# K, V and wo loads issued from GpSimd instead of SyncE in a decode attention kernel

## The chip, the cores and the metric

The kernel runs on one core of a Trainium2 chip. The metric is the device time of one execution in microseconds, as the median of several runs. The profile is one more execution, recorded by the hardware profiler.

## What is computed

Two independent blocks, A and B, of the same shape: one new token for each of two sequences attends over a cache of 8192 keys in 32 heads of width 192. The two results are laid side by side.

```python
B, Sq, D = 2, 1, 640;  H, Sk, Dh = 32, 8192, 192          # all bf16
q = (x @ wq).reshape(B, Sq, H, Dh).transpose(0, 2, 1, 3)
scores = einsum("bhqd,bhkd->bhqk", q, k_cache) * Dh ** -0.5
p = softmax(scores, axis=-1)
o = einsum("bhqk,bhkd->bhqd", p, v_cache)
block = o.transpose(0, 2, 1, 3).reshape(B, Sq, H * Dh) @ wo
out = concatenate([block_A, block_B], axis=-1)
```

Each K and V element is read once, and the two caches of the two blocks are 805 MB of the 837 MB that are read.

## The kernel before

The work is cut into 64 units (`NU`). A unit is one pair of heads of one sequence: head one of the pair lies on partitions 0 to 63, head two on 64 to 127, and each partition holds 128 keys. Its K, and likewise its V, is one transfer of 128 rows of 48 KB, 6144 KB in all.

The transfers go into three buffers (`kv`, buffers 0 to 2 inside the tile `big`), taken in turn in the order of the list `loads`: K0, K1, V0, K2, V1, K3, V2 and so on, and V63 at the end. A load may begin when the load three places before it in the list has been used up (`done(i - NBUF)`): a K is used up when the last of its four multiplies has ended, a V when its PV matmuls have ended. So K(u+2) waits for PV of unit u-1, V(u+1) waits for the last multiply of K(u+1), and K2 waits for the last multiply of K0. K1 and V0 instead wait for the q matmuls of the first and the second block (`("pq", PPB * i - 1)`), because wq of both blocks lies where buffers 1 and 2 will be.

All loads are issued by SyncE in one order: wq of A, x of A and B, wq of B, K0, then the rest of `loads`, then wo in six pieces that go into the same buffers as these come free, then the two outputs.

What the engines do for unit u:

- VectorE multiplies K by q, which is spread over the partitions, in four chunks of 32 keys (`dve_mul`, L285). It reduces what TensorE has summed (`dve_red`, L289), takes the maximum of the scores in each partition (`dve_max`, L295), and finishes the sums of unit u-2 (L300 to L306).
- TensorE sums 192 products to 16 by twelve matmuls with the identity for each chunk (`pe_sum`, L362), then does the 64 PV matmuls of unit u-1 (`pe_pv`, L376).
- GpSimd takes the maximum over the partitions (`pool_ar`, L266, the all-reduce), once for each unit. Before the loops it fills constants.
- ScalarE makes the bias, the exponentials and the scaled outputs (L315, L324, L309).

The order of each engine's instructions comes from the tables `tabs`: `put(engine, slot, order, function, waits, signal)` enters an instruction, and at the end each engine's entries are sorted by slot, then by order. The slot is mostly the unit. SyncE has no table; its instructions run in the order in which they were added to `S_sp`. GpSimd's all-reduce of unit u has slot u and order 0. An engine runs its instructions strictly in order; a wait holds all that follow it.

A transfer adds 16 to a semaphore when it has landed. Before, each of the three buffers has one semaphore (`bsem`), and each load of it waits for the next multiple of 16.

At the start, q of all heads is made by TensorE from x and wq (`pe_q`, L354) and spread by VectorE and ScalarE (L275, L280); at the end wo is applied (`pe_out`, L404).

Of the kernel before, what the change touches and what calls it, by code (L numbers as in the profile page):

```python
# [117 lines left out]
def build_kernel(nc, blocks, out):  # L118
# [15 lines left out]
    NU = NP * B  # L134
    LASTU = NU - 1
    scale = float(Dh) ** -0.5
    NBUF = 3
# [9 lines left out]
    with ExitStack() as es:  # L147
        sb = lambda name, shape, dt: es.enter_context(nc.sbuf_tensor(name, shape, dt))
        ps = lambda name, shape, dt: es.enter_context(nc.psum_tensor(name, shape, dt))
        sem = lambda name: es.enter_context(nc.semaphore(name))  # L150
# [42 lines left out]
        reg = {}  # L193
        S_sp = _Stream("sp", sem("s_sp"), reg)
# [1 line left out]
        S_act = _Stream("act", sem("s_act"), reg)  # L196
        S_dve = _Stream("dve", sem("s_dve"), reg)
        S_pool = _Stream("pool", sem("s_pool"), reg)
        bsem = [sem(f"bsem{i}") for i in range(NBUF)]

        def dsem(k, n=1):
            reg[k] = (sem("d_" + "_".join(str(i) for i in k)), 16 * n)
# [6 lines left out]
        loads = [("k", 0)]  # L209
# [1 line left out]
            loads += [("k", u), ("v", u - 1)]  # L211
        loads += [("v", LASTU)]
        buf = {}
        bcount = [0] * NBUF
        for i, (kind, u) in enumerate(loads):
            buf[kind, u] = i % NBUF
            bcount[i % NBUF] += 1
            reg[(kind, u)] = (bsem[i % NBUF], 16 * bcount[i % NBUF])

        bk, b62, b63 = buf["k", LASTU], buf["v", LASTU - 1], buf["v", LASTU]  # L220
        assert (bk, b62, b63) == (2, 0, 1)
# [1 line left out]
        pieces = []  # L223
        for blk, rows, off, w in ((0, (WR,), woA, [("s", LASTU, NCH - 1)]), (1, (29,), wo0, [("pv", LASTU - 1)]),
                                  (1, (11, 5, 2, 1), wo1, [("pv", LASTU)])):
            r = 29 if off == wo1 else 0
            for n in rows:
                pieces.append((blk, r, r + n, off, w))
                off, r, w = off + n * D, r + n, []
# [9 lines left out]
        def back(name, u, c, n):  # L239
            i = u * NCH + c - n  # L240
            return (name, i // NCH, i % NCH) if i >= 0 else None

        def dma(out_ap, in_ap, k):
            s = reg[k][0]
            return lambda eng: eng.dma_start(out_ap, in_ap).then_inc(s, 16)
# [8 lines left out]
        def ld_wo(n):  # L254
            blk, r0, r1, off, _ = pieces[n]
            src = blocks[blk]["wo"].rearrange("(p i) n -> p (i n)", i=WR)
            return dma(big[:, off:off + (r1 - r0) * D], src[:, r0 * D:r1 * D], ("wo", n))

        def ld_kv(kind, u):
            hp, b = u // B, u % B  # L260
            blk, h = hp // PPB, 2 * (hp % PPB)
            src = blocks[blk][kind][b, h:h + 2].rearrange("s (p t) d -> (s p) t d", p=64)
            return dma(kv[buf[kind, u]], src, (kind, u))
# [154 lines left out]
        def put(eng, slot, order, fn, waits, sig, tag=None):  # L418
            t = tabs[eng].setdefault(slot, [])
            t.append((order, len(t), fn, waits, sig, tag))  # L420
# [14 lines left out]
        for u in range(NU):  # L435
            for c in range(NCH):
                w = [("k", u), ("pq", NP - 1), ("qa", NP - 1), ("qx", NP - 1), back("s", u, c, 2)]
# [32 lines left out]
        for n, p in enumerate(pieces):  # L470
            w = [("wo", n), ("ot", p[0])]
# [8 lines left out]
        def done(i):  # L480
            if i < 0:
                return None
            kind, u = loads[i]
            return ("m", u, NCH - 1) if kind == "k" else ("pv", u)
# [5 lines left out]
        for i, (kind, u) in enumerate(loads):  # L490
            w = [done(i - NBUF)]
            if i in (1, 2):
                w = [("pq", PPB * i - 1)]
            S_sp.add(ld_kv(kind, u), waits=w)
        for n in range(len(pieces)):
            S_sp.add(ld_wo(n), waits=pieces[n][4])
        for blk in range(NBLK):
            S_sp.add(out_dma(blk), waits=[("oev", blk, 1), ("oev", blk, 0)])

# [2 lines left out]
        for n in range(1, HP + 1):  # L502
            S_pool.add((lambda n: (lambda eng: eng.memset(tri[0:n, n:n + 1], 1.0)))(n),
                       waits=[("tri0",)] if n == 1 else [], sig=("tri",) if n == HP else None)
# [5 lines left out]
        for n in range(128 // HP):  # L510
# [3 lines left out]
                  waits=[("id1",), ("place0",)], sig=("place",))  # L514
# [50 lines left out]
def bass_concat_heads__gqa_block_cached__mha_block_cached__decode_kernel(  # L565
    nc: bass.Bass,
    A_x: bass.AP,
    A_k_cache: bass.AP,
    A_v_cache: bass.AP,
    A_wq: bass.AP,  # L570
    A_wo: bass.AP,
    B_x: bass.AP,
    B_k_cache: bass.AP,
    B_v_cache: bass.AP,
    B_wq: bass.AP,
    B_wo: bass.AP,
    out: bass.AP,
):
    blocks = [
        dict(x=A_x, k=A_k_cache, v=A_v_cache, wq=A_wq, wo=A_wo),  # L580
        dict(x=B_x, k=B_k_cache, v=B_v_cache, wq=B_wq, wo=B_wo),
    ]
    build_kernel(nc, blocks, out)
# [28 lines left out]
```

## Time and profile before

| | |
|---|---|
| time before, median of 3 runs | 1937.1 us (1936.89 to 1937.25) |
| the profiled execution, span | 1936.0 us |
| bytes read from HBM | 836.77 MB, 432 GB/s over the span |
| DMA queue of SyncE (q1) | 99.9% of 16 engines' span |
| DMA issues by GpSimd | none |
| TensorE matmul busy | 1545.0 us (80%) |
| VectorE busy | 1124.0 us (58%) |
| GpSimd busy | 28.4 us (1%) |

The page gives the span of the profiled execution; what lies around it is the 1.1 us between the span and the median of the runs. Times in the rows are microseconds from the start of the span. In rows of the timeline the first two numbers are start and duration, the last bracket is how long the engine had been idle and what released it. SPq is SyncE's queue, which issues transfers; such a row lasts as long as the issuing, not the transfer. A row that groups several issues ("x2") reaches from the first to the end of the last. The last number of a row of the list of DMA issues is the median time from issue to landing.

### The profile page before, as it was taken

What the parts mean: (1) busy time and instruction counts of PE and PEld (TensorE: products, weight loads), DVE (VectorE), ACT (ScalarE), POOL (GpSimd) and SP (SyncE); (2) the same over time, 40 slices, a digit from 0 to 9 for tenths busy, and PEclk for the clock granted to TensorE, in tenths of its full rate; (3) what the DMA queues carried; (4) which work ended last, traced back from release to release, by engine and by line L of the source; (5) the groups of instructions that cost most, each with busy time, mean ns of one, the idle gap of its engine ahead of it and who ended that gap; (6) DMA issues with size and microseconds to landing.
All of it is one profiled execution on the core that took longest, in us unless ns stands there. A gap on an engine that the chain in (4) does not pass through costs nothing.

```text
span 1936.0 us, 19059 instructions
## 1 busy us (share of the span) xinstructions
PE 1545.0 (80%) x7728; PEld 743.0 (38%) x7729; DVE 1124.0 (58%) x907; ACT 142.3 (7%) x519; POOL 28.4 (1%) x113
## 2 busy tenths in 40 slices
PE   5777878878878878878878878878878878878878
PEld 2333434434434434434434434433433433433434
DVE  4765565565565565565565565565565565565560
ACT  3100000000000000000000000000000000000000
POOL 0000000000000000000000000000000000000000
PEclk9899989988989988989988999999999999999999
DMA  9999999999999999999999999999999999999999
GB/s 419 427 435 436 432 434 438 430 434 437 434 433 434 437 431 435 437 432 433 436 436 431 434 438 429 436 437 432 434 435 436 430 436 438 428 436 437 433 433 391
DMA packets 19610, 836.91 MB, mean 432 GB/s; under 512 B 2184, under 2 KB 2320, under 8 KB 2576
## 3 DMA queue, kind: packets, MB, share of 16 engines
q1 hardware_dynamic: 19600, 836.78, 99.9%
q8 instruction: 6, 0.10, 0.0%
q14 instruction: 4, 0.03, 0.0%
HBM read 836.77 MB, written 0.01 MB: 432 GB/s over the span
## 4 chain that ended last, share of the span: by engine, by line
DMA 49%; PE 31%; DVE 17%; issue 3%; DVEq 0%; SPq 0%; ACT 0%; ACTq 0%
DMA big<-in_B_k_cache_dram 24%; DMA big<-in_A_k_cache_dram 22%; PE ops L376 18%; DVE big L285 15%; PE scps L362 12%; DMA big<-in_B_wq_dram 2%; DVE sc L289 1%; DMA big<-in_B_wo_dram 1%; PE scps L354 0%; PE ops L368 0%; PE outps L354 0%; DVEq L285 0%; DVE qall L275 0%; PE scps L404 0%; PE oTps L390 0%
## 5 line engine op out<-in xcount | busy, mean ns | idle before, releaser
L285 DVE TENSOR_TENSOR big<-big,qall 128x6144 bf16<-128x6144 bf16 x256 | 852.7, 3351 | 490.7 <-DMA big<-in_B_k_cache_dram 260.6
L362 PE MATMUL scps<-big,ident 128*128 128x512 bf16 x3072 | 815.6, 426 | 358.2 <-DVE big L285 355.7
L376 PE MATMUL ops<-big,pb 128*34 128x384 bf16 x4096 | 676.8, 326 | 0.0
L362 PEld LDWEIGHTS scps<-big,ident 128*128 128x128 bf16 x3072 | 314.3, 107 | 852.7 <-DVE big L285 439.2
L376 PEld LDWEIGHTS ops<-big,pb 128*34 128x34 bf16 x4096 | 395.5, 98 | 258.7
L289 DVE TENSOR_REDUCE sc<-scps 128x32 f32<-128x512 f32 x256 | 175.9, 687 | 227.7 <-PE scps L362 227.7
L315 ACT ACTIVATE nb<-mg 64x1 f32<-64x1 f32 x128 | 25.8, 201 | 1707.7 <-POOL mg L266 1706.9
L324 ACT ACTIVATE pb<-sc,nb 64x128 bf16<-64x128 f32 x128 | 55.8, 436 | 7.8
L266 POOL PARTITION_ALL_REDUCE mg<-mp x64 | 25.7, 402 | 1859.1 <-DVE mp L295 1859.1
L295 DVE TENSOR_REDUCE mp<-sc 64x1 f32<-64x128 f32 x128 | 35.9, 280 | 8.3
L309 ACT ACTIVATE qall<-o_sum,rc 2x192 f32 (+1 forms) x64 | 29.0, 453 | 20.7 <-DVE o_sum L306 19.1
L306 DVE TENSOR_TENSOR o_sum<-ops,o_hi 2x192 f32<-2x192 f32 x64 | 22.1, 346 | 7.7
L354 PE MATMUL scps<-big,xw 128*128 x120 | 23.2, 351 | 2.6 <-DVE xw L271 2.2
L324 ACT ACTIVATION_READ_ACCUMULATOR pb<-sc,nb 64x1 f32 x128 | 23.7, 185 | 0.0
L303 DVE COPY o_hi<-ops 2x192 f32<-2x192 f32 x64 | 22.3, 349 | 2.0
L300 DVE RECIPROCAL rc<-ops 2x1 f32<-2x1 f32 x64 | 10.0, 156 | 21.3 <-PE ops L376 19.3
L275 DVE CAST qall<-scps 64x192 f32 x48 | 17.0, 355 | 7.2 <-PE scps L354 5.4
L280 ACT ACTIVATE qall<-scps 64x192 f32 x48 | 15.6, 324 | 30.5 <-DVE qall L275 28.2
L345 PE MATMUL oTps<-ident,xw 4*128 4x4 bf16 x5 | 0.4, 178 | 21.5 <-DMA xw<-in_B_x_dram 21.5
L354 PEld LDWEIGHTS scps<-big,xw 128*128 128x128 bf16 x120 | 12.4, 103 | 12.1 <-issue 5.9
L368 PEld LDWEIGHTS ops<-ones,rs 128*2 128x2 f32 x128 | 5.5, 82 | 26.9 <-issue 26.9
L404 PE MATMUL outps<-big,oT 128*2 128x320 bf16 x96 | 9.2, 369 | 4.6 <-DMA big<-in_A_wo_dram 4.6
(36 smaller groups left out, 67.6 us busy)
## 6 DMA issues: line engine op xcount, KB each, us to landing
big<-in_A_k_cache_dram SPq DMA_DIRECT2D x32, 6144.0 KB, 28.6
big<-in_A_v_cache_dram SPq DMA_DIRECT2D x32, 6144.0 KB, 27.6
big<-in_B_k_cache_dram SPq DMA_DIRECT2D x32, 6144.0 KB, 28.9
big<-in_B_v_cache_dram SPq DMA_DIRECT2D x32, 6144.0 KB, 27.8
big<-in_A_wq_dram SPq DMA_DIRECT2D x1, 7680.0 KB, 21.2
big<-in_B_wq_dram SPq DMA_DIRECT2D x1, 7680.0 KB, 38.2
big<-in_A_wo_dram SPq DMA_DIRECT2D x1, 7680.0 KB, 29.0
big<-in_B_wo_dram SPq DMA_DIRECT2D x1, 4640.0 KB, 29.3
```

Of the source, the lines that this page charges most:

```text
L266: return lambda eng: eng.partition_all_reduce(mg[u % 3][:], mp[u % 3][:], 128, bass.bass_isa.ReduceOp.max)
L285: return lambda eng: eng.tensor_tensor(prod[c % 2], t[:, c * TC:(c + 1) * TC, :], qall[:, S_dve.at(u), :].broadcast_to([128, TC, Dh]), ALU ...
L289: return lambda eng: eng.tensor_reduce(sc[u % 3][:, c * TC:(c + 1) * TC], scps[(u * NCH + c) % 3][:], AXL.X, ALU.add)
L295: ins = eng.tensor_reduce(mp[u % 3][r, s:s + 1], sc[u % 3][r, :], AXL.X, ALU.max)
L303: return lambda eng: eng.tensor_copy(o_hi[:], ops[u % 3][32:34, Dh:QW])
L306: return lambda eng: eng.tensor_tensor(o_sum[:], ops[u % 3][0:2, 0:Dh], o_hi[:], ALU.add)
L309: return lambda eng: eng.activation(qall[0:2, S_act.at(u), :], o_sum[:].unsqueeze(1), ACTF.Identity, scale=rc[u % 3][:])
L315: ins = eng.activation(nb[u % 3][r, :], mg[u % 3][r, s:s + 1], ACTF.Identity, scale=-scale)
L324: ins = eng.activation(dst, sc[u % 3][r, :].rearrange("p (g j a) -> p g a j", j=JB, a=2), ACTF.Exp, bias=nb[u % 3][r, :], scale=scale, acc ...
L354: ins = eng.matmul(qps[hp % NQ][:, 0:QW], xbc[:, blk, c, :], wq_t[blk][:, c, S_pe.at(off, QW, QW)], start=(c == 0), stop=(c == DC - 1))
L362: ins = eng.matmul(scps[(u * NCH + c) % 3][:], ident[:], prod[c % 2][:, :, j * DG:(j + 1) * DG], start=(j == 0), stop=(j == NJ - 1))
L376: ins = eng.matmul(ops[u % 3][0:MP, 0:QW], pb[u % 3][:, j0s:j0s + MP], vv[:, j, :], start=(j == 0), stop=(j == TJ - 1))
```

## The change

All loads but the first five are issued by GpSimd. SyncE keeps wq of A, the two x, wq of B, K0, and the two outputs. K1 and all later K, all V, and the six pieces of wo are entered in GpSimd's table: K(u) in slot u-2 with order 3, behind the all-reduce of unit u-2; V(u) in slot u with order -1, ahead of the all-reduce of unit u; wo in slot 64, behind the last all-reduce. The waits are the same as before. GpSimd's order becomes: fills, K1, V0, all-reduce 0, K2, V1, all-reduce 1, K3, V2, all-reduce 2, and so on, all-reduce 62, V63, all-reduce 63, wo in six pieces.

The buffers and their order are the same. Each buffer has two semaphores, one for loads issued by SyncE and one for those issued by GpSimd; of the first kind only the one of buffer 0 is used, by K0. The loops of the other engines keep their instructions; a register step moves by one place in two of them.

```diff
-        bsem = [sem(f"bsem{i}") for i in range(NBUF)]
+        bsem = [[sem(f"bsem{i}_{n}") for i in range(NBUF)] for n in range(2)]
...
-        bcount = [0] * NBUF
+        bcount = [[0] * NBUF for _ in range(2)]
+
+        def queue(i):
+            kind, u = loads[i]
+            return 0 if i == 0 else 1
+
         for i, (kind, u) in enumerate(loads):
+            q = queue(i)
             buf[kind, u] = i % NBUF
-            bcount[i % NBUF] += 1
-            reg[(kind, u)] = (bsem[i % NBUF], 16 * bcount[i % NBUF])
+            bcount[q][i % NBUF] += 1
+            reg[(kind, u)] = (bsem[q][i % NBUF], 16 * bcount[q][i % NBUF])
...
             if i in (1, 2):
                 w = [("pq", PPB * i - 1)]
-            S_sp.add(ld_kv(kind, u), waits=w)
+            if queue(i) == 0:
+                S_sp.add(ld_kv(kind, u), waits=w)
+            elif kind == "k":
+                put("pool", u - 2, 3, ld_kv(kind, u), w, None)
+            else:
+                put("pool", u, -1, ld_kv(kind, u), w, None)
         for n in range(len(pieces)):
-            S_sp.add(ld_wo(n), waits=pieces[n][4])
+            put("pool", NU, n, ld_wo(n), pieces[n][4], None)
```

## The prediction

> **What bounds the kernel now.** I read the page first (engines, slices, DMA), then who waits for whom on SyncE's queue, then the timeline of a unit in the middle, of the start and of the end.
>
> ```profile
> span 1936.0 us, 19059 instructions
> PE 1545.0 (80%) x7728; PEld 743.0 (38%) x7729; DVE 1124.0 (58%) x907; ACT 142.3 (7%) x519; POOL 28.4 (1%) x113
> DMA  9999999999999999999999999999999999999999
> q1 hardware_dynamic: 19600, 836.78, 99.9%
> ...
> 100.00:500.00 400.00, 324.86 (x1584) 154.94 (x1582) 238.97 (x182) 25.93 (x98) 4.96 (x14) 0.93 1.00 434
> 54.00:69.00 15.00, 8.50 (x29) 3.25 (x30) 12.10 (x8) 1.20 (x4) 0.00 (x0) 0.77 0.99 427
> ```
>
> The one queue that carries all loads keeps the 16 DMA engines busy for 99.9% of the span; a long window in the middle has a DMA share of 1.00 at 434 GB/s (last column), with no slice below nine tenths. No compute engine is above 80%. So the time is bytes divided by rate, plus whatever time the DMA engines stand idle, which today is next to nothing. The change moves no byte more or less. It can cost time only by leaving the DMA engines without a queued load, or by a software-fed queue that moves bytes at another rate.
>
> How much early the loads are issued is seen in one unit:
>
> ```profile
> 985.60 0.33 SPq L245 DMA_DIRECT2D big<-in_B_v_cache_dram  x1
> 989.91 0.35 POOL L266 PARTITION_ALL_REDUCE mg<-mp  x1 [29.46 <-DVE mp L295]
> 998.02 6.63 DVE L285 TENSOR_TENSOR big<-big,qall 128x6144 bf16<-128x6144 bf16 x2 [7.17 <-DMA big<-in_B_k_cache_dram]
> 999.05 0.33 SPq L245 DMA_DIRECT2D big<-in_B_k_cache_dram  x1
> 1013.78 0.33 SPq L245 DMA_DIRECT2D big<-in_B_v_cache_dram  x1
> 1027.01 3.36 DVE L285 TENSOR_TENSOR big<-big,qall 128x6144 bf16<-128x6144 bf16 x1 [7.97 <-DMA big<-in_B_k_cache_dram]
> ...
> big<-in_B_k_cache_dram SPq DMA_DIRECT2D x32, 6144.0 KB, 28.9
> big<-in_B_v_cache_dram SPq DMA_DIRECT2D x32, 6144.0 KB, 27.8
> ```
>
> K lands every 1027.01 - 998.02 = 29.0 us, so one load takes 14.5 us. From issue to landing are 28.9 and 27.8 us: each load is issued about 28.9 - 14.5 = 14.4 us (K) or 13.3 us (V) before its own turn. An issue may come that much later before the DMA engines feel it.
>
> **Steady state: the issue itself.** 127 K and V loads leave SyncE (0.33 us each there, which nothing waits for) and go to GpSimd. The trace of before has no transfer issued by GpSimd, so its price is bounded: below by SyncE's 0.33 us, above by the longest GpSimd instruction there is, 3.42 us (quoted below). Either is within the 13.3 us. In GpSimd's order V(u) now stands ahead of the all-reduce of unit u, and K(u+2) behind it. V went out at 985.60 and the all-reduce began at 989.91: 4.3 us of room, more than 3.42. Were it late, ScalarE's exponential of that unit would be late, whose PV matmuls run only a unit (29 us) later. K(u+2) waits for PV of u-1, at 999.05, long after the all-reduce at 989.91, so the all-reduce holds up nothing there. Cost: nothing, hidden by the 13 us; without that cover, 0.3 to 3.4 us for each of 127 issues. The second set of semaphores adds no instruction to the loops beyond a register step. Cost nothing.
>
> **The end.**
>
> ```profile
> 1886.20 0.33 SPq L245 DMA_DIRECT2D big<-in_A_wo_dram  x1
> 1887.69 0.35 POOL L266 PARTITION_ALL_REDUCE mg<-mp  x1 [28.49 <-DVE mp L295]
> 1896.83 14.25 SPq L245 DMA_DIRECT2D big<-in_B_wo_dram  x5
> big<-in_A_wo_dram SPq DMA_DIRECT2D x1, 7680.0 KB, 29.0
> big<-in_B_wo_dram SPq DMA_DIRECT2D x1, 160.0 KB, 23.2
> ```
>
> The first wo load now goes behind the last all-reduce: 1887.69 + 0.35 = 1888.04 instead of 1886.20, 1.8 us later. It needs 7.86 MB / 434 GB/s = 18.1 us of its 29.0, so it has 10.9 us to spare. The last, smallest piece (160 KB, under 1 us of transfer) is issued by 1896.83 + 14.25 = 1911.08 and lands 23.2 us after issue; four pieces at up to 3.4 us each, 13.7 us, still fit. The outputs stay on SyncE. Cost nothing.
>
> **The start.** Here I see a cost. K0 stays on SyncE's queue, K1 and V0 go to the other.
>
> ```profile
> 1.81 0.36 SPq L245 DMA_DIRECT2D big<-in_B_wq_dram  x1
> 2.21 38.04 SPq L245 DMA_DIRECT2D big<-in_A_k_cache_dram  x2
> 21.49 0.35 PE L345 MATMUL oTps<-ident,xw 4*128 4x4 bf16 x5 [21.49 <-DMA xw<-in_B_x_dram]
> 53.74 0.33 SPq L245 DMA_DIRECT2D big<-in_A_v_cache_dram  x1
> 55.58 6.63 DVE L285 TENSOR_TENSOR big<-big,qall 128x6144 bf16<-128x6144 bf16 x2 [0.99 <-ACT qall L280]
> 71.95 0.33 SPq L245 DMA_DIRECT2D big<-in_A_k_cache_dram  x1
> 77.18 3.42 POOL L266 PARTITION_ALL_REDUCE mg<-mp  x1 [73.94 <-DVE mp L295]
> 89.39 0.33 SPq L245 DMA_DIRECT2D big<-in_A_v_cache_dram  x1
> ...
> big<-in_B_wq_dram SPq DMA_DIRECT2D x1, 7680.0 KB, 38.2
> big<-in_A_k_cache_dram SPq DMA_DIRECT2D x1, 6144.0 KB, 52.3
> big<-in_A_k_cache_dram SPq DMA_DIRECT2D x1, 6144.0 KB, 29.8
> big<-in_A_v_cache_dram SPq DMA_DIRECT2D x1, 6144.0 KB, 30.7
> ...
> q1 hardware_dynamic: 48, 2.36, 91.5%
> q14 instruction: 1, 0.01, 0.3%
> ```
>
> The four loads are the second wq, K0, K1 and V0, with times from issue to landing. The second wq lands at 1.81 + 38.2 = 40.0; K0 at 2.21 + 52.3 = 54.5, right behind it; K1, issued at 2.21 + 38.04 - 0.33 = 39.9, at 69.7; V0 at 53.74 + 30.7 = 84.4. All in the order of issue: within one queue a transfer waits its turn, as the tiny x did, which held PE until 21.49.
>
> The last fence's final two rows are the DMA queues between 76 and 82 us: while V0 (and K2 behind it) filled q1, one packet of q14 went through. A queue of its own does not wait for another queue's backlog. So K1, ready 39.9 us in, would no longer stand behind K0 but share the engines with it. I take even shares, since the q14 packet was let in at once though q1 had far more waiting, and put the case of no share among the rivals. If K1's first bytes move at 39.9 + g, K0 has 14.6 - g left at half speed and lands at 69.1 - g instead of 54.5. The Trainium skill, "DMA: Bandwidth & Descriptors", section Queues, rings and completion order, says that each DMA engine takes turns between the queues that have work, a packet at a time. By that rule the shares would be even, which gives the sum below; the one q14 packet agrees, though it only shows that another queue is let in, and by it alone the delay lies anywhere between none and that sum.
>
> A packet is a row of 48 KB (6144 KB in 128 rows, 8 for each engine, 14.5 / 8 = 1.8 us). Having begun first, K0 finishes about half a packet, 0.9 us, sooner.
>
> What this sets off: all K0 work on DVE starts later. From the first multiply to the all-reduce of unit 0 are 77.18 - 55.58 = 21.6 us of DVE and PE work that stays. In before, K2 was issued at 71.95, as soon as K0's last multiply had ended, 16.4 us after the first. In GpSimd's new order K2 stands behind that all-reduce, and so waits for 21.6 us and its 3.42 us. Its first bytes need g again:
>
> (69.1 - g - 0.9) + 21.6 + 3.42 + g = 93.2 us.
>
> g cancels. K0, K1 and V0 together are the same bytes, moved without a pause, so V0 still ends at 84.4. From 84.4 to 93.2 nothing is queued: **8.8 us** of idle DMA engines. Nothing gives them back, since the rest of the kernel runs at the DMA rate.
>
> Does a second gap follow? K2 lands at 93.2 + 14.5 = 107.7. V1 waits for K1's last multiply, 89.39 in before, 33.8 us after the first multiply of K0; now 68.2 - g + 33.8 = 102.0 at most. In time, by 5.7 us, against a g of up to 3.42 + about 1. From there each load has the steady lead again.
>
> Bounds of the 8.8: the all-reduce at the steady 0.35 instead of 3.42 us gives 5.7; a first GpSimd issue that is slow and the later one quick takes off 3.1, so 2.6 at least; the reverse adds 3.1, so 11.9.
>
> **The sum.** Steady 0, end 0, start +8.8. The profiled execution has a span of 1936.0 us, so 1944.8; the median of the runs is 1937.1, 1.1 above the span, so **1945.9 us**, +0.45%. With the bounds, 1939.7 to 1949.0.
>
> **Rivals.**
>
> 1. K0 keeps its place (no gain, not slower). If the engines go on with K0's packets, which were queued long before, until they are done, K0 lands at 54.5, the all-reduce runs at 77.18 as before and ends at 80.6; K2 then goes out 3.8 us before V0 ends at 84.4. The gap is gone if K2's g is under 3.8: 1937.1 us. It decides from the share that K0 keeps: with all of it 0, with half 8.8. The gap opens once K0 lands later than 55.6 + 3.8 - g (before 55.6 the first multiply waits for q, not for K0). For it: K0's descriptors all stand in q1 39.9 us in. Against: the q14 packet that was let in.
>
> 2. The software-fed queue is slower per byte. It carries 127 x 6144 KB plus 2 x 7680 KB, 814.7 MB of 836.78. At 434 GB/s that is 1877 us; at the 427 of the window from 54 to 69, the poorest I take as a bound for a full queue, 1908: 31 us more, 1937.1 + 8.8 + 31 = 1977. Each 0.1 us of seam between loads costs 12.7 us, so 0.3 us per load would also bring 1984. For it: such a load is in no row of before. Against: packets of 48 KB and a lead of 13 us leave little for a slower feed to show. The Trainium skill, same page, section Measured, has 425 GB/s for 16 MB loads issued from GpSimd; by it the loads take 1917 us, 40 more, and the sum would be 1986. No row here shows it.
>
> 3. The new queue is a little faster per byte. To pay for 8.8 us, 814.7 MB would have to move at 434 x 1877 / 1868 = 436.0 GB/s or more. At 438, the highest slice of the page, 1860 us, 17 less: 1929. Against: 434 holds over 400 us with nothing idle.
>
> ```profile
> GB/s 419 427 435 436 432 434 438 430 434 437 434 433 434 437 431 435 437 432 433 436 436 431 434 438 429 436 437 432 434 435 436 430 436 438 428 436 437 433 433 391
> ```
>
> Slices of 438 stand beside slices of 428, which says that a slice holds one landing more or less, not that the rate moves.
>
> **How the numbers follow.** About 0.2% (3.9 us) can be told from no change. Forecast, a gap at the start: 0.58, of which nearly all is over 3.9 us. Rival 1: 0.17, within 0.2%. Rival 2: 0.17, slower. Rival 3: 0.08, faster. So faster 0.08, same 0.18, slower 0.74. The range takes in rival 1 and the forecast's bounds, and the mild end of rival 2 (0.1 us of seam on top, 1958.6): 1936 to 1958, which leaves out about 0.2.
>
> **What would show it.** In the trace of after: K0's landing about 65 to 68 instead of 54.5 us, the first multiply with it; GpSimd's first all-reduce near 90; K2's issue right behind it; the second of the 40 DMA slices (48 to 97 us) at about 8, the rest at 9; 434 GB/s in the middle; K landing every 29.0 us. It is wrong if K0 lands at 54.5, if the middle's rate is not 434, or if waits for K grow beyond the 8 us of before.

## The result, and the profile after

The changed kernel takes 1949.44 us (median of 3 runs, 1947.3 to 1949.48) against 1937.1 us: a ratio of 1.0060, interval 1.0045 to 1.0074. It is slower by 0.6%, as forecast; the forecast was 1945.9 us. A second set of five runs on another occasion gave 1947.95 us (1946.95 to 1949.09), ratio 1.0057 (1.0043 to 1.0071). The loss is 12.3 us in the first set and 10.7 in the second, where the forecast had 8.8; the first median lies 0.4 us above the 1949.0 where the bounds of the forecast's sum ended, the second within them. The profiled execution took 1947.3 us, with a span of 1945.6, 9.6 longer than before.

The page after, its span, DMA slices and queues:

```profile
span 1945.6 us, 19038 instructions
DMA  9899999999999999999999999999999999999999
GB/s 420 346 431 435 436 434 433 434 434 435 436 434 435 433 433 435 436 434 435 434 433 434 437 431 436 434 434 435 435 433 435 435 433 435 435 433 435 435 433 387
q0 software_dynamic: 18992, 814.75, 96.8%
q1 hardware_dynamic: 448, 22.03, 2.6%
```

The loads of GpSimd are the queue q0. One slice of forty is below 9, the second, at 346 GB/s where it was 427. Two stretches of the changed kernel (start and end, length, busy time of TensorE's matmuls, its weight loads, VectorE, ScalarE and GpSimd, granted TensorE clock, DMA share, GB/s) show the hole and the rate in the middle:

```profile
84.00:91.00 7.00, 4.69 (x16) 1.83 (x16) 5.89 (x6) 1.03 (x5) 3.83 (x2) 0.76 0.00 1
500.00:900.00 400.00, 309.68 (x1578) 150.83 (x1579) 233.53 (x181) 25.94 (x98) 19.92 (x42) 0.97 1.00 434
```

From 84 to 91 us the DMA engines stand still; in the middle the rate is 434 GB/s, as before. The timeline of the changed kernel around the hole (the helper that issues loads is now L251, the multiply L291, the all-reduce L272):

```profile
39.51 0.68 POOL L251 DMA_DIRECT2D big<-in_A_k_cache_dram  x1 [36.26 <-PE outps L360]
53.89 0.54 POOL L251 DMA_DIRECT2D big<-in_A_v_cache_dram  x1 [13.70 <-PE outps L360]
65.32 6.63 DVE L291 TENSOR_TENSOR big<-big,qall 128x6144 bf16<-128x6144 bf16 x2 [10.87 <-DMA big<-in_A_k_cache_dram]
86.47 3.41 POOL L272 PARTITION_ALL_REDUCE mg<-mp  x1 [32.04 <-DVE mp L301]
89.75 0.55 POOL L251 DMA_DIRECT2D big<-in_A_k_cache_dram  x1
98.81 0.53 POOL L251 DMA_DIRECT2D big<-in_A_v_cache_dram  x1 [8.51 <-DVE big L291]
107.66 6.63 DVE L291 TENSOR_TENSOR big<-big,qall 128x6144 bf16<-128x6144 bf16 x2 [4.99 <-DMA big<-in_A_k_cache_dram]
```

These are K1, V0, the first multiply of K0, the all-reduce of unit 0, K2, V1, and the first multiply of K2. The first multiply has waited 10.87 us for K0 and starts at 65.32 instead of 55.58. K2 goes out at 89.75, directly after the all-reduce. Its data are there at 107.66, 8.7 us later than the 98.95 of before (71.95 + 27.0). The lists of DMA issues in this stretch (K0, K1, V0, K2; last number from issue to landing):

```profile
big<-in_A_k_cache_dram SPq DMA_DIRECT2D x1, 6144.0 KB, 63.0
big<-in_A_k_cache_dram POOLq DMA_DIRECT2D x1, 6144.0 KB, 29.3
big<-in_A_v_cache_dram POOLq DMA_DIRECT2D x1, 6144.0 KB, 30.5
big<-in_A_k_cache_dram POOLq DMA_DIRECT2D x1, 6144.0 KB, 17.9
```

K0, issued at 2.2, lands at 65.2 instead of 54.5; K1 at 39.51 + 29.3 = 68.8 (before 69.7); V0 at 84.4, unchanged. K2 lands 17.9 us after issue, where a load in the middle takes 28: no other load was ahead of it.

### The profile page after: what moved, and what is told of

The parts are those of the page before. It is cut to its first block, busy times and chain, and to the rows that moved or that the text cites. A ratio compares the mean times of both kernels' runs of the same rounds, so it can differ in the third digit from the quotient of the medians.

```text
span 1945.6 us, 19038 instructions
## 1 busy us (share of the span) xinstructions
PE 1528.3 (79%) x7728; PEld 737.3 (38%) x7729; DVE 1123.0 (58%) x907; ACT 142.4 (7%) x519; POOL 99.4 (5%) x246
## 4 chain that ended last, share of the span: by engine, by line
DMA 47%; PE 32%; DVE 17%; issue 4%; another core or an unknown queue 1%; DVEq 0%; ACT 0%; SPq 0%; POOL 0%; ACTq 0%
DMA big<-in_B_k_cache_dram 23%; DMA big<-in_A_k_cache_dram 22%; PE ops L382 18%; DVE big L291 15%; PE scps L368 12%; DVE sc L295 1%; DMA big<-in_B_wo_dram 1%; DMA xw<-in_B_x_dram 1%; PE scps L360 1%; PE outps L360 0%; PE ops L374 0%; DVE qall L281 0%; DVEq L291 0%; PE scps L410 0%
## 5 line engine op out<-in xcount | busy, mean ns | idle before, releaser
L291 DVE TENSOR_TENSOR big<-big,qall 128x6144 bf16<-128x6144 bf16 x256 | 852.9, 3352 | 510.5 <-DMA big<-in_A_k_cache_dram 268.4
L368 PE MATMUL scps<-big,ident 128*128 128x512 bf16 x3072 | 800.0, 419 | 383.5 <-DVE big L291 381.2
L368 PEld LDWEIGHTS scps<-big,ident 128*128 128x128 bf16 x3072 | 308.9, 106 | 867.8 <-DVE big L291 459.4
L251 POOL DMA_DIRECT2D big<-in_B_v_cache_dram x32 | 16.9, 529 | 477.8 <-DVE big L291 450.2
L251 POOL DMA_DIRECT2D big<-in_A_v_cache_dram x32 | 16.9, 528 | 468.9 <-DVE big L291 455.2
L272 POOL PARTITION_ALL_REDUCE mg<-mp x64 | 25.4, 397 | 265.4 <-DVE mp L301 265.4
L251 POOL DMA_DIRECT2D big<-in_A_k_cache_dram x31 | 17.0, 550 | 299.0 <-PE ops L382 262.8
L251 POOL DMA_DIRECT2D big<-in_B_k_cache_dram x32 | 17.5, 545 | 289.7 <-PE ops L382 289.7
```

What stands on the lines that cost most here:

```text
L272: return lambda eng: eng.partition_all_reduce(mg[u % 3][:], mp[u % 3][:], 128, bass.bass_isa.ReduceOp.max)
L291: return lambda eng: eng.tensor_tensor(prod[c % 2], t[:, c * TC:(c + 1) * TC, :], qall[:, S_dve.at(u), :].broadcast_to([128, TC, Dh]), ALU ...
L368: ins = eng.matmul(scps[(u * NCH + c) % 3][:], ident[:], prod[c % 2][:, :, j * DG:(j + 1) * DG], start=(j == 0), stop=(j == NJ - 1))
```

## The experiments

Each was timed against the kernel before on the same chip, and each is an edit of the changed kernel unless it says otherwise.

**Is it the sharing, or the place of K2?** Two edits, each of which undoes one half of the story. The first puts K2 ahead of the all-reduce:

```diff
-                put("pool", u - 2, 3, ld_kv(kind, u), w, None)
+                put("pool", u - 2, -0.5 if u == 2 else 3, ld_kv(kind, u), w, None)
```

> The queues as in the changed kernel, but K2 stands ahead of the first all-reduce in GpSimd's order, not behind it. Theory: K0 still lands near 65 us, shared with K1; K2 is issued when K0's last multiply ends, near 81, and its first bytes come 1.3 us later, before V0 ends at 84.4: no gap, 1936.5 to 1940 us. Rival (the sharing itself or the delay of K0 costs, whatever the order): 1944 to 1949 us.

Measured: 1942.01 us (1941.19 to 1942.69), ratio 1.0024 (1.0015 to 1.0034). More than half of the loss is gone, but not all of it; my range ended at 1940. K2 and V1 in its timeline:

```profile
81.84 0.53 POOL L251 DMA_DIRECT2D big<-in_A_k_cache_dram  x1 [27.48 <-DVE big L291]
99.29 0.55 POOL L251 DMA_DIRECT2D big<-in_A_v_cache_dram  x1 [9.05 <-DVE big L291]
```

and a stretch at V1's issue:

```profile
98.00:102.00 4.00, 2.95 (x15) 1.29 (x16) 1.74 (x3) 0.00 (x0) 0.55 (x1) 1.00 0.67 197
```

K2 is issued at 81.84, ahead of V0's landing near 84.4, but that is still a little late, because a load counts as landed only when the slowest of the 16 engines is through with it. These are the DMA slices of this kernel from 82 to 86 us; a packet counts in the slice in which it begins, and a packet is a row of 48 KB:

```profile
DMA  0000000000999990090099000000000090999999
```

From 82.0 to 83.0 no row begins, and the engines that are through with V0 stand idle; K2's first rows begin at 83.0, 1.2 us after its issue. The next load, V1, is later still: it waits for the last multiply of K1, which came as late as all the rest, and goes out at 99.29 when K2 is landing at 81.84 + 18.0 = 99.8. The rate from 98 to 102 is 197 GB/s. Together the two gaps make the first multiply of K4 start 4.4 us later than before (table below), of 5.0 us in the span. In the changed kernel the gap at V1 was covered, because K2 itself was late. So the delay of K0 reaches two later loads, and closing the gap at the first opens one at the second.

The other half: K1 stays where it is in GpSimd's order, but waits for the q matmuls of the second block, so that K0 has landed when it comes.

```diff
-                w = [("pq", PPB * i - 1)]
+                w = [("pq", NP - 1)]
```

> The queues and the order as in the changed kernel, but K1 waits for the q matmuls of the second block, as V0 does, and so is issued near 53.7 us, when K0 has nearly landed. Theory: K0 lands at 54.5; K1 has nothing to share with. If its first bytes come 1.3 us after issue, no gap to speak of: 1937 to 1939 us. If the first transfer that GpSimd issues needs the 4.9 us that K1's issue needed in the changed kernel, a gap of up to 4 us near 55: 1941 to 1943 us. Rival (the sharing is not the cause): 1945 to 1949 us.

Measured: 1940.58 us (1940.14 to 1940.95), ratio 1.0016 (1.0007 to 1.0025), between the two ranges that the theory gave. Without the sharing the first multiply starts at 55.40 again and the hole at 84 is gone, although K2 still stands behind the all-reduce. What is left is another gap, between K0's end and K1's first bytes. K1's issue, from the timeline:

```profile
53.84 0.68 POOL L251 DMA_DIRECT2D big<-in_A_k_cache_dram  x1 [50.59 <-PE outps L360]
```

and the DMA slices from 51 to 55 us and from 54 to 57 us:

```profile
DMA  0099999999990000000000000000000000000000
DMA  0000000000000000999900099000000000000000
```

K0's last rows begin by 52.2, and K1's first in the slice at 55.2, 1.4 us after issue; in between no row begins. The first multiply of K4 is 2.6 us later than before, of 2.9 us in the span. The 4.9 us that I feared for the first transfer of GpSimd were not needed here.

**Other ways to divide the first loads.** K1 back on SyncE, by the function `queue`:

```diff
-            return 0 if i == 0 else 1
+            return 0 if i <= 1 else 1
```

> K1 goes back to SyncE's queue, V0 and all that follows stay on GpSimd's. Theory (two queues share the engines, and K2 stands behind the first all-reduce): K0 lands at 54.5 us as in the kernel before, but now V0, issued at 53.9, shares with K1, which lands near 81 instead of 69.7. VectorE's first multiply of K1 stands ahead of its last reduce of unit 0, so the all-reduce starts near 85 and K2's first bytes come near 90: a gap again, of 5 to 6 us, and 1944 to 1948 us in all. Rival (only the delay of K0 costs): no gap, 1937 to 1939 us.

Measured: 1946.48 us (1945.78 to 1946.64), ratio 1.0048 (1.0034 to 1.0061).

```profile
80.40 3.36 DVE L291 TENSOR_TENSOR big<-big,qall 128x6144 bf16<-128x6144 bf16 x1 [7.68 <-DMA big<-in_A_k_cache_dram]
85.17 3.41 POOL L272 PARTITION_ALL_REDUCE mg<-mp  x1 [30.53 <-DVE mp L301]
88.45 0.57 POOL L251 DMA_DIRECT2D big<-in_A_k_cache_dram  x1
```

and a stretch:

```profile
84.00:91.00 7.00, 5.97 (x21) 2.38 (x22) 5.82 (x6) 1.40 (x6) 3.85 (x2) 0.69 0.38 112
```

K0 is on time (its first multiply starts at 55.52), and there is a hole all the same, with 112 GB/s from 84 to 91 us: now K1 shares with V0, VectorE waits 7.68 us for it at 80.40, and the all-reduce behind it (85.17, foreseen near 85) holds K2. The rival, that only K0's delay costs, falls.

K0, K1 and V0 on SyncE:

```diff
-            return 0 if i == 0 else 1
+            return 0 if i <= 2 else 1
```

> K0, K1 and V0 all on SyncE's queue, K2 and all that follows on GpSimd's. Theory: the first three land in order, at 54.5, 69.7 and 84.4 us; the all-reduce ends near 80.6, K2's first bytes come near 82, before V0 ends; no gap, 1936.5 to 1939 us. What is left above 1937.1 is what the GpSimd queue costs outside the start. Rival (the queue fed by GpSimd is slower per byte or per load): 1945 us or more, and less than 434 GB/s in the middle.

Measured: 1939.19 us (1938.09 to 1940.17), ratio 1.0011 (1.0002 to 1.0020), just above the 1939 where the expected range ended. The all-reduce is at 76.21, K2 goes out at 79.49, and no stretch of the start has a hole. The timeline:

```profile
76.21 3.40 POOL L272 PARTITION_ALL_REDUCE mg<-mp  x1 [72.97 <-DVE mp L301]
79.49 0.70 POOL L251 DMA_DIRECT2D big<-in_A_k_cache_dram  x1
```

and two stretches:

```profile
84.00:91.00 7.00, 5.90 (x31) 2.55 (x30) 4.70 (x4) 0.00 (x0) 0.54 (x1) 1.00 1.04 449
500.00:900.00 400.00, 307.66 (x1560) 148.34 (x1559) 237.41 (x176) 24.07 (x91) 19.57 (x41) 0.97 1.00 434
```

K0 on GpSimd as well, so that no K shares with a K:

```diff
-            return 0 if i == 0 else 1
+            return 1
```

> The changed kernel with K0 on GpSimd's queue as well, so that all K and V loads are one queue in order, and nothing of K shares with K. K0 then shares with both wq from the start: wq of A lands near 33 us instead of 21, wq of B near 54 instead of 39, q is ready 14 us later, and the first multiply starts near 70 us. Theory (what counts is when the first multiply starts, since 21.6 us of work and the all-reduce lie between it and K2): a gap of about 12 us, 1949 to 1954 us. Rival (what cost was K1 and K0 in two queues): 1938 to 1941 us.

Measured: 1951.70 us (1950.75 to 1952.56), ratio 1.0076 (1.0062 to 1.0090), in the middle of what the theory gave, though it is slower than the changed kernel itself. The first multiply and K2's issue:

```profile
69.82 6.63 DVE L291 TENSOR_TENSOR big<-big,qall 128x6144 bf16<-128x6144 bf16 x2 [0.99 <-ACT qall L286]
93.80 0.55 POOL L251 DMA_DIRECT2D big<-in_A_k_cache_dram  x1
```

and the issues of both wq:

```profile
big<-in_A_wq_dram SPq DMA_DIRECT2D x1, 7680.0 KB, 33.6
big<-in_B_wq_dram SPq DMA_DIRECT2D x1, 7680.0 KB, 52.4
```

Now K0 takes its share from wq (33.6 and 52.4 us to landing instead of 21.2 and 38.2), q is late, and the first multiply, at 69.82, waits for q instead of K0. K2 is later still.

**Does the queue that GpSimd feeds cost something by itself?** Only K1 on GpSimd, all else on SyncE, wo too:

```diff
-            return 0 if i == 0 else 1
+            return 1 if i == 1 else 0
-            put("pool", NU, n, ld_wo(n), pieces[n][4], None)
+            S_sp.add(ld_wo(n), waits=pieces[n][4])
```

> Only K1 on GpSimd's queue; K0 and everything else on SyncE's, so that K2 does not stand behind the all-reduce. Theory (K1 in another queue delays K0 by 10 us; K2 then comes just in time, but V1, which waits for K1's last multiply near 99 us, comes at or after the end of K2's transfer): a seam near 99 us of about 2 us, 1939.5 to 1941 us. Rival (the 4.7 us that were left with K2 ahead of the all-reduce come from the queue that GpSimd feeds): 1937.2 to 1937.8 us.

Measured: 1941.89 us (1941.58 to 1943.85), ratio 1.0026 (1.0017 to 1.0035); above both ranges (the theory's ended at 1941, the rival's at 1937.8). One load in the other queue costs as much as 127 loads and wo in it, with K2 ahead of the all-reduce (1942.01). The same two gaps are there; V1's issue, at the second:

```profile
99.63 0.33 SPq L251 DMA_DIRECT2D big<-in_A_v_cache_dram  x1
```

and the stretch:

```profile
98.00:102.00 4.00, 2.90 (x14) 1.16 (x13) 2.20 (x2) 0.00 (x0) 0.00 (x0) 1.00 0.68 209
```

So feeding the other 126 loads and wo from GpSimd costs nothing that these runs can tell: 1942.01 against 1941.89, with intervals of about 0.1% each. The traces say it more sharply: in both kernels what they are later than before is the same at K4 and at the last K, to 0.01 us (table below).

**The 1.9 us left with three loads on SyncE.** I thought of the small wo pieces at the end. wo alone on GpSimd, as an edit of the kernel before:

```diff
-            S_sp.add(ld_wo(n), waits=pieces[n][4])
+            put("pool", NU, n, ld_wo(n), pieces[n][4], None)
```

> The kernel before, with only the six wo loads issued by GpSimd. Theory (the tail costs the 1.9 us): 1938.5 to 1939.5 us. Rival (the tail is covered, as forecast): 1937.0 to 1937.6 us.

Measured: 1937.47 us (1937.09 to 1939.03), ratio 1.0003 (0.9994 to 1.0012): by the median the rival, and the forecast of the end, hold. But three of the eleven runs took 1939.0, 1.5 us more than the median, where none of the 21 runs of before took more than 1937.52; what was different in them is not known, since the profiled run was not one of the three. The reverse, K0, K1, V0 and wo on SyncE, the other loads on GpSimd:

```diff
-            return 0 if i == 0 else 1
+            return 0 if i <= 2 else 1
-            put("pool", NU, n, ld_wo(n), pieces[n][4], None)
+            S_sp.add(ld_wo(n), waits=pieces[n][4])
```

> K0, K1 and V0 on SyncE's queue, and the six wo loads too; only K1's successors K2 to K63 and V1 to V63 on GpSimd's. Theory (the 1.9 us that were left with the first three loads on SyncE come from the last, small wo pieces, which land later or are seen later when GpSimd issues them): 1937 to 1938 us. Rival (they come from the 125 K and V loads themselves): 1938.5 to 1940 us.

Measured: 1941.78 us (1938.45 to 1944.68), ratio 1.0023 (1.0014 to 1.0032): more, not less, and outside both expectations. The eleven runs spread over 6.2 us. The timeline of the profiled one, 1941.09 us, shows:

```profile
1869.13 0.55 POOL L251 DMA_DIRECT2D big<-in_B_v_cache_dram  x1 [9.05 <-PE ops L382]
1885.91 0.33 SPq L251 DMA_DIRECT2D big<-in_A_wo_dram  x1
1908.93 11.93 PE L382 MATMUL ops<-big,pb 128*34 128x384 bf16 x64 [10.86 <-DMA big<-in_B_v_cache_dram]
```

It is the start over again. V63 is issued at 1869.13, the first wo load at 1885.91 on the other queue, where it no longer waits behind V63; V63 lands late, PE waits 10.86 us for it, and the last PV matmuls end at 1920.9, when wo should be in use (from 1915.28 in the kernel before).

The last try put loads 20 to 109 on GpSimd and kept start, end and wo on SyncE:

```diff
-            return 0 if i == 0 else 1
+            return 1 if 20 <= i < 110 else 0
-            put("pool", NU, n, ld_wo(n), pieces[n][4], None)
+            S_sp.add(ld_wo(n), waits=pieces[n][4])
```

> Loads 20 to 109 of the 128 (K and V of units 10 to 54) on GpSimd's queue, the start, the end and wo on SyncE's. If a load that GpSimd issues costs something in itself (1.9 us for 125 of them), 1938.4 to 1938.9 us; if it costs nothing in the steady state, and the 1.9 us come from the start and the end, 1937.0 to 1937.8 us. At the change of queues two loads share for a while, which the lead of 13 us should cover.

Measured: 1944.02 us (1942.83 to 1944.93), ratio 1.0034 (1.0021 to 1.0046), outside both again. It does not answer its question, since each change of queue costs a gap of its own. At the first change:

```profile
342.57 6.63 DVE L291 TENSOR_TENSOR big<-big,qall 128x6144 bf16<-128x6144 bf16 x2 [19.41 <-DMA big<-in_A_k_cache_dram]
```

and the stretches at both:

```profile
355.00:366.00 11.00, 9.56 (x51) 4.70 (x52) 8.60 (x11) 1.86 (x7) 0.88 (x2) 1.00 0.86 340
1660.00:1672.00 12.00, 9.49 (x49) 4.18 (x47) 9.42 (x10) 0.29 (x2) 0.35 (x1) 1.00 0.86 348
```

Where the queue changes, a K shares with the V that follows it in the list, VectorE waits 19.41 us for this K (7.17 and 7.97 in the unit of before), and the next V is issued too late: 340 GB/s over 11 us and 348 over 12 where the middle has 434, so about 2.4 us of transfer are missing at each change, 4.8 of the 6.7 us in all. The lead of 13 us did not cover the sharing, although I had expected it to.

Where the 1.9 us come from stays open in the main. The profiled run of the kernel with three loads on SyncE has 1.3 of them in its span: 0.8 are there at K4, although no stretch before it has a hole, and 0.4 come after the last K, where TensorE waits for the last pieces of wo:

```profile
1934.90 0.57 PE L410 MATMUL scps<-big,oT 128*2 128x320 bf16 x6 [1.16 <-DMA big<-in_B_wo_dram]
```

In the kernel before the last such wait is 0.71 us. With the three slow runs of wo alone on GpSimd this makes wo a suspect, not a shown cause. The rate in the middle is the same.

The changed kernel once more:

> The changed kernel once more, beside the others: 1946.5 to 1949.5 us, with a gap of about 8 us near 84 us in its profile. It is the measure for the next three on the same chip, and shows whether the 2.2 us between its first three runs come back.

Measured: the 1947.95 us given above. This is as expected, and the same hole is there (0.00 of DMA share from 84 to 91 us). The five runs spread over 2.1 us, where those of before spread over less than 0.6. What makes them spread was not found.

## Why the prediction was right

**Steady state, cost nothing: held.** GpSimd needs 0.53 to 0.55 us for an issue, near the lower bound of 0.33, and the middle runs at 434 GB/s. GpSimd's waits and its longer issues are covered: what is lost is lost by K4, and the 118 loads from K4 to the last K add nothing. The rows of the first multiply of K4 and of the last K, each after and then before, are

```profile
166.28 6.63 DVE L291 TENSOR_TENSOR big<-big,qall 128x6144 bf16<-128x6144 bf16 x2 [8.16 <-DMA big<-in_A_k_cache_dram]
157.11 6.63 DVE L285 TENSOR_TENSOR big<-big,qall 128x6144 bf16<-128x6144 bf16 x2 [8.11 <-DMA big<-in_A_k_cache_dram]
1877.20 6.63 DVE L291 TENSOR_TENSOR big<-big,qall 128x6144 bf16<-128x6144 bf16 x2 [7.14 <-DMA big<-in_B_k_cache_dram]
1868.01 6.63 DVE L285 TENSOR_TENSOR big<-big,qall 128x6144 bf16<-128x6144 bf16 x2 [8.23 <-DMA big<-in_B_k_cache_dram]
```

The same two rows of the other profiled runs, as us later than before:

| kernel | K4 | last K | end of the span |
|---|---|---|---|
| changed | 9.17 | 9.19 | 9.6 |
| K2 ahead of the all-reduce | 4.39 | 4.38 | 5.0 |
| K1 issued late | 2.64 | 2.69 | 2.9 |
| K1 on SyncE | 8.04 | 8.06 | 7.9 |
| K0, K1 and V0 on SyncE | 0.79 | 0.86 | 1.3 |
| K0 on GpSimd too | 13.23 | 13.22 | 13.3 |
| only K1 on GpSimd | 4.46 | 4.47 | 4.6 |

**The end, cost nothing: held.** The kernel with wo alone on GpSimd is the same as before within its interval; in the changed kernel the end adds 0.4 us (9.6 at the end of the span against 9.2 at the last K).

**The start, +8.8 us: the mechanism held, but the number came out so close because errors in it cancelled.** Steps, predicted and measured: the first multiply 68.2 - g, measured 65.32; 21.6 us to the all-reduce, measured 21.15; the all-reduce 3.42, measured 3.41 in length with K2 issued 3.28 after its start; V0's landing 84.4, measured 84.4. But g is not the same twice, so it does not cancel. These are the DMA slices of the changed kernel from 43.5 to 45.5 us and from 88 to 92:

```profile
DMA  0000000000009990990099999090990000000000
DMA  0000000000000000000000000000009999090900
```

K1's first rows begin in the slice at 44.1, 4.6 us after issue. K2's begin at 91.0, 1.25 us after issue. The even shares were right. These are the two queues from 44 to 62.2 us:

```profile
q1 hardware_dynamic: 80, 3.93, 49.9%
q0 software_dynamic: 80, 3.93, 49.9%
```

K0 has 54.5 - 44.1 = 10.4 us left when K1 comes in, so with half a packet taken off it should have landed at 54.5 + 10.4 - 0.9 = 64.0. It landed at 65.2. A load ends with one short packet on each engine, and these had to take their turn too. Here is queue q1, which still has K0 alone, from 61.5 to 64 us and from 64 to 65:

```profile
q1 hardware_dynamic: 1, 0.00, 0.0%
q1 hardware_dynamic: 15, 0.00, 0.8%
```

After 61.5 no row of K0 begins any more, so its rows have ended by 63.3; 15 of its 16 short packets come only after 64, each behind one more row of K1. That the last packet of a load waits its turn was not in the forecast.

K2's first bytes came at 91.0 instead of 93.2, since the second g was 3.0 us smaller than the first (4.2, counted from the 39.9 of the forecast); the later landing of K0, less the shorter steps behind it, took 0.7 of that back. This alone would make the idle time 6.6 us. But it did not begin at 84.4. These are the slices from 80 to 84 us, and the queue from 90.9 to 91.9:

```profile
DMA  0099999999999000000090000000000000000000
q0 software_dynamic: 16, 0.79, 255.9%
```

V0's last rows begin between 80.2 and 81.3, one at 82.0, and take 1.8 us each: on the mean of the 16 engines V0 is over at 82.7, and only the slowest engine makes the landing 84.4. K2's first rows begin at 91.3 on the mean. So an engine stood idle for 8.6 us, and its first row after that took 2.56 us (255.9% of 1 us) instead of 1.8, another 0.7. That makes 9.3, and K4 is 9.2 later than before. Two steps of the forecast were thus off by about 2 us each and in opposite directions: g, which should have cancelled, and the landing of V0, which was taken for the end of its transfers. That they came to 8.8 was luck.

It would be wrong to find a cost of restarting in the 16.6 us that K2 needs from its first bytes to its landing. The 14.5 us of a load in a full queue are the time between two landings. In the kernel before, V0's 16 short packets and K2's first 16 rows behind them begin between 82.3 and 84.05 us,

```profile
DMA packets 32, 0.79 MB, mean 449 GB/s; under 512 B 16, under 2 KB 16, under 8 KB 16
```

and K2 lands at 98.95, 16.6 us after the first of them as well.

**No second gap: held, by its margin.** V1 went out at 98.81, foreseen for 102.0 - g = 97.8 at most, ahead of K2's landing at 107.66. With K2 ahead of the all-reduce the margin is gone, and the gap at V1 appears.

**The sum** gave 1944.8 for the span and 1945.9 for the median. The span was 1945.6: 9.2 + 0.4 against 8.8. Around the span lie 1.7 us instead of 1.1, and the median lies 2.1 above the profiled run. Those 2.7 us, and the 1.9 of the kernel without a hole, were in no term of the sum.

**The rivals.** K0 did not keep its place (65.2, not 54.5). The rule of the Trainium skill ("DMA: Bandwidth & Descriptors", Queues, rings and completion order), turns of one packet each, agrees with what the trace shows: 80 packets of q0 and 80 of q1 while K0 and K1 shared, and K0 landing 10.7 us later. The rate of 425 GB/s for GpSimd's loads that the same page gives in Measured is not what these 48 KB rows show: 434 in both kernels. By the same 434 the new queue was neither slower nor faster.

## What to carry to other kernels

When a kernel is bound by its loads, one queue in order is also a priority: the load that is needed first comes first. Moving the later of two loads to a second queue takes bandwidth from the earlier one, and whatever waits for that one, and for what follows from it, is late; look for the next loads that wait on it, since closing one gap may open the next. Count the engines as idle from the end of their last packets, not from the landing of the load: here that was 1.7 us earlier. A load whose own wait has long been satisfied should not stand behind an instruction with a longer wait on the same engine.

## What the runs showed of the hardware

A load in a second queue had its first bytes 1.2 to 1.4 us after issue where the engines stood idle, but 4.6 us after it while another queue kept them busy, about two packets of 1.8 us more. V0 in the kernel with K1 on SyncE, issued at 53.97 and begun at 58.5, needed the same; the first wo load on SyncE beside GpSimd's queue, issued at 1885.91 and begun at 1889.3, needed 3.4. From then on the two queues took even turns, and the short packet at the end of a load took its turn as well, behind a row of the other queue. After the pause of 8.6 us an engine's first row took 2.56 us instead of 1.8; beyond this 0.7 us no cost of the pause shows. The issue itself took GpSimd 0.53 to 0.55 us in the steady state (0.68 for its first), where SyncE took 0.33.
